# Both heads of a pair take their raw-score maxima from different row halves of TensorE, k gets eight slots, and the order is set anew

## The chip, the cores and the metric

One core of one Trainium2 chip runs the whole program. The metric is the device time of one execution in microseconds (us). TensorE multiplies matrices, VectorE and GpSimd do elementwise work and reductions, ScalarE does activations and copies, and SyncE issues the DMAs. In the profile these are PE (PEld for its weight loads), DVE, POOL, ACT and SP.

## The reference, cut to what matters

```python
def _attn_ref(q, k, v, g_q, g_k):                      # 4 batches, 12 heads, 448 rows, 64 wide
    q_n, k_n = (rmsnorm(q, g_q), rmsnorm(k, g_k))
    scores = scale * np.matmul(q_n, k_n.transpose(0, 1, 3, 2))
    scores = scores - np.max(scores, axis=-1, keepdims=True)
    attn = np.exp(scores)
    attn = attn / (np.sum(attn, axis=-1, keepdims=True) + 1e-09)
    return np.matmul(attn, v)

def reference(...):
    x = attn_out                        # as 1792 tokens by 768
    x = _moe_ref(x, phi, w1, w2)        # soft mixture of 8 experts, 4 slots each
    return _moe2_ref(x, w_in, w_out)    # h = x @ w_in; (h * sigmoid(1.702 h)) @ w_out
```

The change is in the attention alone. The experts and the last two products follow it and are the same in both kernels.

## The kernel before, in words

The 48 heads are worked through as 24 pairs of heads. Two pairs make a quad, which is what one load of q, k or v brings. For each pair `square` and `meansq` give the mean squares, `invert` gives 1/rms, `gain` and `normalise` scale q and k, and then each of q and k is split into a high and a low 16-bit half (`q_hi`, `q_lo`, `k_hi`, `k_lo`, with copies in `q_again` and `k_again`). A slot is 128 columns wide: 64 of them hold the high half of 64 numbers, the other 64 the low half or a helper. q has eight slots in a pair (four chunks of rows for each of two heads). k has seven: three full chunks for each head, and one slot in which the last 64 rows of both heads share the 128 partitions.

`turn` transposes such a tile by a DMA that SP issues. Pairs 0 and 1 use TensorE instead (`pe_turn`, `pe_copy`). After the transpose the 64 numbers of a high half lie on 64 of TensorE's 128 rows. The transposed tiles are KBT (k high and a -1), QAT (q high and low), KAT (k low and high) and QBT (q high and the maximum).

A pair is then handled in two steps. First `mx` multiplies the high halves of q and k, 64 rows deep, and `mx_max` takes the maximum over the 448 keys on VectorE, straight from PSUM. It works in groups: three groups of two chunks each (two matmuls of 128 columns against 448, into two PSUM banks, and one reduction over 2 x 448), and a fourth group for the last 64 rows of both heads, whose two matmuls of 64 columns write partitions 0 to 63 and 64 to 127 of one bank, with one reduction over 448. `mx_move` then carries the second head's maxima from partitions 64 to 127 down to 0 to 63. There is one PSUM buffer for these groups (`mx=1` in `BUFS`), so a group's matmuls wait until the reduction of the group before is done. Pair 0 takes its chunks one by one from the score buffers, in seven groups. Second, once the maxima are written into the q tile and that is transposed (`tqb`), `sc` makes the scores in two 128-row matmuls for each chunk, `sc_exp` exponentiates on ScalarE, `esum` adds for the denominators, and `pv`, `sums`, `xst` and `xmul` make the rows that the mixture of experts reads.

The order of all this is written by `run`, a planner inside the kernel: each step is an `op` with an engine, a cost and a due time, and the planner lists the steps on every engine when the program is built. The tables `ON` (which of DVE, POOL or ACT does a step of a pair, one letter for each pair), `SHIFT` (what is added to a due time) and `COST` steer it. On the chip each engine then runs its list in order, and waits at the head of the list for what the next step needs. Where the planner expects TensorE to be idle it puts in small filler matmuls (`warm`, line 366). Weights for the experts are loaded ahead during the attention (`early`), and into the attention's own buffers as these come free at its end (`ev`, `e0` to `e3`).

Around it stand the loads of the quads on SP (lines 372 and 376), the transposes on SP (line 472), the maxima on PE (line 506) and DVE (line 510), `mx_move` (line 517) and the scores (line 525).

Of the kernel before, what the change touches and what calls it, by code (L numbers as in the profile page):

```python
# [20 lines left out]
def soft_moe_block_kernel(  # L21
# [21 lines left out]
    C = 4  # L43
# [11 lines left out]
        gain="PPPPPDPDPPPPPPPPDDPDPPDD",  # L55
        qn="DPPPPDPPPPPPPPPPPPPDPPPP",
        kn="DPDDDDDDPPPDPPDDPDPDPPPP",
        qlo="PPPPPPPDPPPPPDPPDPDPDDDD",
        klo="PDPDPPPPPPDDPPPPPPDDPDDP",
        q2="DADPADADDPAAPDPAAAAADAAP",  # L60
        k2="DDDADAAADADAPPADDDPAAPPP",
        e01="DPPPPPPDPPDPPDPPDDPPDDDD",
        e02="DPPPDPPPPDPPDPDDDPDDDPPP",
        e11="PPPPPDDPDDPPDDPPPDPPPPPD",
        e12="PPPPPPPPPDPPDPPPDDDPDPPP",
        x0="DADDAAAAADDDAAAADDDDADDD",
        x1="AAADDDDDDAADAAAADDADDAAA",
        nr="DDDDPPPPPPPP",
# [137 lines left out]
    tmp_t = wr_t[0][:, 2048:3008].rearrange("p (a d) -> p a d", d=D)  # L206
# [22 lines left out]
    rings["rstd"] = [w3_t[:, 2976 + 32 * i:3006 + 32 * i] for i in range(2)]
# [25 lines left out]
        e0=2528.9, e1=-318.3, e2=1377.8, e3=-312.5, early=-356.6, esum=1121.5, ev=683.3, exp=101.7,  # L255
        gain=2452.3, guard=-280.1, invert=-347.4, k2=1399.8, khi=-233.2, klo=-1664.4, kn=1136.3, lk=404.5,
        logits=-430.7, lq=-148.4, max=32.7, meansq=-234, move=-828, mx=-239.9, out=-2170.8, pe_tka=-148.1,
        pe_tkb=-423.3, pe_tqa=279.8, pe_tqb=-458.7, pv=-92.3, q2=144.5, qhi=379.1, qlo=-547.3, qn=1645.5,
        r_add=1029.5, r_back=78.3, r_eb=512.8, r_exp=-422.8, r_fade=-274.5, r_gather=-1334.2, r_max=-104.7,
        r_more=-342.3, r_neg=51.3, r_old=-38.4, r_turn=-770.3, r_z=23.8, recip=-482, sc=149.1, square=-302.9,  # L260
        squarek=-1386.1, ssb=-423.4, sumT=-108.1, sums=-696.5, tka=1788, tka0=-596.3, tkb=-430.1, tkb0=981,
        tqa=-351.3, tqa0=-100.1, tqb=-605.9, tqb0=-2095.7, v=1218.9, w_back=-205.6, w_copy=-1379.6,
        w_exp=-467.5, w_guard=385.6, w_max=-49.2, w_neg=-638.7, w_recip=416.3, w_scale=1218.5, w_sel=-46.1,
        w_sum=1102.3, w_turn=-561.7, w_z=-432.7, x=1755.3, xmul=372.4,
    )
    COST = dict(
        gain=(0.6, 1.23), qn=(0.6, 1.02), kn=(0.53, 0.9), qlo=(0.6, 1.12), klo=(0.53, 1.0), q2=(0.2, 1.1, 0.52),
        k2=(0.19, 1.0, 0.47), e01=(0.53, 1.09), e02=(0.53, 1.09), e11=(0.53, 1.09), e12=(0.53, 1.09),
# [124 lines left out]
    def square(p, i):  # L393
        if i == 0:
            sqt[p] = tmp_t
        nc.scalar.activation(out=sqt[p][:, 8:] if i else sqt[p][:, :8], in_=rows(p, i), func=AF.Square, scale=D ** -0.5)  # L396

    def meansq(p):
        if p % 2 == 0:
            ssqt[p // 2] = new("ssq", [P, 30])  # L400
        nc.vector.tensor_reduce(out=part(ssqt, p, 1), in_=sqt.pop(p), axis=AX.X, op=ALU.add)

    def part(tiles, p, n):

        a = 15 * (p % 2)
        return tiles[p // 2][:, a:a + 15 * n]

    def invert(p, i, n):

        qd = p // 2  # L410
        if i == 0 and p % 2 == 0:
            y0t[qd], ntt[qd] = new("y0", [P, 30]), new("nt", [P, 30])
        if i == 5 and p % 2 == 0:
            rst[qd] = new("rstd", [P, 30])
# [19 lines left out]
    def rows(p, i):  # L434
        a = 8 * (p % 2)
        return of(raw_t, p // 2)[:, i, a:a + 8 - i]
# [7 lines left out]
    def normalise(p, i):  # L444
        n, eng, m = rows(p, i), on("kn" if i else "qn", p)[0], (8, 7)[i]
        r = part(rst, p, 1)[:, 8 * i:8 * i + m].rearrange("p (a o) -> p a o", o=1)
        eng.tensor_tensor(out=n, in0=n, in1=r.to_broadcast([P, m, D]), op=ALU.mult)  # L447
# [1039 lines left out]
```

## Time and profile before

| what | value |
|---|---|
| median of 3 runs | 692.09 us (691.33 to 695.41) |
| the profiled execution's own time | 693.83 us |
| its span | 692.1 us |
| mean granted TensorE clock, as a share | 0.968 |

The profiled execution is one more run than the three. Its time has 1.73 us around the span. The attention runs to about 300 us of the span, the experts to about 415 us, and the last two products to the end.

### The profile page before, as it was taken

To read this page: it belongs to the slowest core of one execution; us is meant where nothing else is said; L and a number is where in the kernel's file an instruction comes from. 1 tells how busy PE (TensorE), PEld (TensorE's weight loads), DVE (VectorE), ACT (ScalarE), POOL (GpSimd) and SP (SyncE) were. 2 spreads that over 40 slices of the span, in tenths; PEclk is the share of its full clock that TensorE was granted. 3 is DMA by queue.
4 is the path that set the end of the run, shared out by engine and by line. 5 is a ranking of instruction groups with operands and counts; after the bars stand their busy time and mean duration, and the time that the engine had idled before them with its cause. 6 is when DMAs were issued, how large, how long until landed. Compare 5 with 4: busy or idle time off the path is not lost.

```text
span 692.1 us, 11043 instructions
## 1 busy us (share of the span) xinstructions
PE 630.0 (91%) x4089; PEld 414.5 (60%) x4089; DVE 377.5 (55%) x640; ACT 365.8 (53%) x762; POOL 191.9 (28%) x233
## 2 busy tenths in 40 slices
PE   1889999999999999989743899999999999999997
PEld 0423434434433433455421335799999999999997
DVE  4997777877887888243544613799511211211211
ACT  2756977877787964532533511898513432333332
POOL 4756898776577353400000010000000000000000
PEclk9999999999999999988966899999999999999999
DMA  8289999898899899659899995663100100100101
GB/s 225 71 166 219 201 225 203 169 224 194 183 213 202 174 217 223 229 192 391 325 407 406 407 357 208 246 223 124 70 0 1 69 1 1 68 1 1 69 0 46
DMA packets 146166, 120.30 MB, mean 174 GB/s; under 512 B 102048, under 2 KB 126880, under 8 KB 146112
## 3 DMA queue, kind: packets, MB, share of 16 engines
q1 hardware_dynamic: 143024, 109.47, 57.7%
q10 hardware_dynamic: 3024, 10.03, 3.7%
q8 instruction: 32, 0.52, 0.3%
q14 instruction: 22, 0.18, 0.1%
q0 software_dynamic: 64, 0.10, 0.1%
HBM read 92.18 MB, written 5.51 MB: 141 GB/s over the span
## 4 chain that ended last, share of the span: by engine, by line
PE 74%; DMA 12%; DVE 9%; ACT 2%; issue 1%; SPq 1%; POOL 0%; ACTq 0%; DVEq 0%; POOLq 0%
PE y L1307 27%; PE y L1324 7%; PE sc L525 7%; PE pv L544 7%; PE mx L506 4%; DMA wr<-in_moe_w_dram 4%; PE pv L539 3%; DMA wr<-wr 3%; PE so_ps L1110 2%; PE h L1077 2%; DVE wr L510 2%; PE f L1266 2%; DMA wt<-in_moe_w_dram 2%; PE ms L591 2%; PE ms L590 1%; DVE wr L447 1%
## 5 line engine op out<-in xcount | busy, mean ns | idle before, releaser
L1288 DVE TENSOR_TENSOR gl<-gg,gh 128x384 fp32r<-128x384 f32 (+1 forms) x80 | 42.2, 530 | 149.1 <-ACT gh L1283 148.3
L510 DVE TENSOR_REDUCE wr<-mx 128x2 f16<-128x896 f32 x92 | 89.7, 975 | 25.5 <-PE mx L506 25.1
L1274 ACT ACTIVATE gg<-f 128x384 f32<-128x384 f32 (+1 forms) x78 | 36.5, 469 | 121.0 <-PE f L1266 120.8
L1307 PE MATMUL y<-wo,gh 128*128 128x384 f32 x352 | 75.4, 335 | 0.0
L532 POOL TENSOR_TENSOR es<-es,e 128x448 f32<-128x448 f32 x47 | 55.4, 1189 | 29.7 <-DVE es L532 12.1
L529 ACT ACTIVATE e<-sc,esc 128x448 f32<-128x448 f32 x96 | 56.6, 637 | 11.5 <-PE sc L525 10.6
L1307 PEld LDWEIGHTS y<-wo,gh 128*128 128x128 f32 x352 | 62.1, 188 | 0.0
L1307 PE MATMUL y<-wh,gl 128*128 128x384 f32 x176 | 46.8, 337 | 0.0
L1307 PE MATMUL y<-wl,gh 128*128 128x384 f32 x176 | 46.7, 336 | 0.0
L1307 PE MATMUL y<-wh,gh 128*128 128x384 f32 x176 | 46.7, 336 | 0.0
L1307 PE MATMUL y<-wo,gl 128*128 128x384 f32 x176 | 44.9, 335 | 0.0
L1283 ACT ACTIVATE gh<-gg 128x384 fp32r<-128x384 f32 (+1 forms) x78 | 39.3, 504 | 7.5 <-PE y L1307 4.2
L396 ACT ACTIVATE wr<-wr 128x512 f32<-128x512 f32 (+1 forms) x48 | 28.6, 604 | 26.5 <-DMA wr<-in_k_dram 12.6
L529 ACT ACTIVATE es<-sc,esc 128x448 f32<-128x448 f32 x54 | 32.9, 634 | 18.3 <-PE sc L525 18.1
L146 ACT ACTIVATE wi<-wst 128x512 f32<-128x512 f32 x24 | 16.2, 675 | 36.4 <-DMA wr<-in_moe_w_dram 15.7
L447 POOL TENSOR_TENSOR wr<-wr 128x512 f32<-128x512 f32 (+1 forms) x33 | 32.8, 1016 | 5.4 <-DVE wr L432 4.9
L525 PEld LDWEIGHTS <-wr 128*128 128x128 f16 (+1 forms) x224 | 18.9, 104 | 24.7 <-issue 17.6
L506 PE MATMUL mx<-wr 64*128 64x448 f16 (+1 forms) x120 | 31.0, 365 | 2.5 <-DVE wr L510 2.4
L143 DVE SCALAR_TENSOR_TENSOR wst<-wst 128x512 uint32<-128x512 uint32 x24 | 16.6, 691 | 28.8 <-ACT wst L149 26.3
L1307 PEld LDWEIGHTS y<-wl,gh 128*128 128x128 f32 x176 | 32.0, 188 | 0.0
L1307 PEld LDWEIGHTS y<-wh,gl 128*128 128x128 f32 x176 | 32.0, 188 | 0.0
L1307 PEld LDWEIGHTS y<-wo,gl 128*128 128x128 f32 x176 | 31.8, 188 | 0.0
(270 smaller groups left out, 1362.7 us busy)
## 6 DMA issues: line engine op xcount, KB each, us to landing
wr<-in_moe_w_dram SPq DMA_DIRECT2D x30, 512.0 KB, 8.7
wt<-in_moe_w_dram SPq DMA_DIRECT2D x24, 512.0 KB, 7.9
wr<-in_moe_w_out_dram SPq DMA_DIRECT2D x15, 768.0 KB, 4.5
wst<-in_moe_w_in_dram ACTq DMA_DIRECT2D x19, 512.0 KB, 7.4
wr<-in_moe_w_dram SPq DMA_DIRECT2D x20, 384.0 KB, 5.5
wt<-in_moe_w_dram SPq DMA_DIRECT2D x20, 384.0 KB, 7.8
out_dram<-o SPq DMA_DIRECT2D x13, 384.0 KB, 2.3
wr<-in_q_dram SPq DMA_DIRECT2D x12, 384.0 KB, 4.7
```

Source lines behind the costliest of these rows:

```text
L447: eng.tensor_tensor(out=n, in0=n, in1=r.to_broadcast([P, m, D]), op=ALU.mult)
L506: nc.tensor.matmul(out, q_cols(QAT[p], h, c)[:D], k_cols(KBT[p], h)[:D], start=True, stop=True)
L510: nc.vector.tensor_reduce(out=of(qb_t, p)[:, at[0]:at[-1] + 1:max(1, at[-1] - at[0]), D:D + 1], in_=MX.pop((p, g))[:, :len(at), :S], axis= ...
L525: nc.tensor.matmul(out, k_cols(a, n, c), q_cols(b, n), start=first, stop=not first)
L529: nc.scalar.activation(out=E[p, h, c], in_=SC.pop((p, h, c)), func=AF.Exp, scale=esc)
L532: on(f"e{h}{c}", p)[0].tensor_tensor(out=E[p, h, 0], in0=E[p, h, 0], in1=E[p, h, c], op=ALU.add)
L544: nc.tensor.matmul(PV[p][h * D:(h + 1) * D, :], t[:, 6 * n + 3 * h + c], E[p, h, c], start=(c == 0), stop=False)
L1274: nc.scalar.activation(out=ggt[w][:, :w[1]], in_=src[:, :w[1]], func=AF.Silu, scale=1.702)
L1283: nc.scalar.activation(out=gh[:, :w[1]], in_=ggt[w][:, :w[1]], func=AF.Copy)
L1288: nc.vector.tensor_tensor(out=G[w][1][:, :n], in0=ggt[w][:, :n], in1=G[w][0][:, :n].bitcast(F32), op=ALU.subtract)
L1307: nc.tensor.matmul(Y[t, u][:, :384], a[:, ts], b[f][:, u * 384:(u + 1) * 384], start=(f == 0 and i == 0), stop=(f == KF - 1 and i == 2),)
L1324: nc.tensor.matmul(Y[t, u][:, :384], a[:, t * 128:(t + 1) * 128], b[:, u * 384:(u + 1) * 384], start=(f == 0 and j == 0), stop=(f == KF - ...
```

## The change

All of q and k now has eight slots in a pair. The first head keeps its high half in columns 0 to 63 of a slot and its low half in 64 to 127; the second head has them the other way round (`lanes`). After the transposes the first head's high halves lie on rows 0 to 63 and the second head's on rows 64 to 127. A group of maxima (pairs 1 to 23) is now one chunk of both heads: two matmuls, one on each half of TensorE's rows, into two PSUM banks, and one reduction over 2 x 448. The last group has 64 rows of each head, on partitions 0 to 63, and reduces 2 x 448 too. `mx_move` goes. Pair 0 has eight groups of one chunk. k's tiles, squares and copies grow from 448 to 512 columns and its two transposed tiles from 7 to 8 blocks, and the short load of k becomes one DMA in a quad instead of two. Small tiles (1/rms and its helpers, the gain, the 16-bit identity) move to the buffer `wv`, so that the last of the `ev` loads waits for more steps and the last loads of `e2` and `e3` for fewer. The tables `ON`, `SHIFT` and `COST` have new numbers.

```diff
@@ ON, SHIFT, COST (one row of each shown) @@
-        kn="DPDDDDDDPPPDPPDDPDPDPPPP",
+        kn="DDPPDPDDPPDDDPDDDPDPPDPP",
-        logits=-430.7, lq=-148.4, max=32.7, meansq=-234, move=-828, mx=-239.9, out=-2170.8, pe_tka=-148.1,
+        lq=-482.3, max=3.6, meansq=-561.7, mx=-361.9, out=-2747.4, pe_tka=-741.5, pe_tkb=1475.9, pe_tqa=1239.5,
-        gain=(0.6, 1.23), qn=(0.6, 1.02), kn=(0.53, 0.9), qlo=(0.6, 1.12), klo=(0.53, 1.0), q2=(0.2, 1.1, 0.52),
+        gain=(0.6, 1.23), qn=(0.6, 1.02), kn=(0.6, 1.02), qlo=(0.6, 1.12), klo=(0.6, 1.12), q2=(0.2, 1.1, 0.52),
...
-        load(qd, k, t[:, :, :3], [(t[h * SH:(h + 1) * SH, 0:4:2, 3], slice(h, 4, 2)) for h in range(2)])
+        load(qd, k, t[:, :, :3], [(t[:SH, :, 3], slice(0, 4))])
...
-        return of(raw_t, p // 2)[:, i, a:a + 8 - i]
+        return of(raw_t, p // 2)[:, i, a:a + 8]
+    def heads(x):
+        return x.rearrange("p (h c) d -> p h c d", h=2)
+    def lanes(t, second):
+        at, step = (D, 448) if second else (0, 576)
+        flat = t.rearrange("p a d -> p (a d)")
+        return bass.AP(flat.tensor, flat.offset + at, [list(flat.ap[0]), [step, 2], [128, C], [1, D]])
...
-        nc.scalar.activation(out=of(kb_t, p)[:, :, 0:D], in_=rows(p, 1), func=AF.Copy)
+        nc.scalar.activation(out=lanes(of(kb_t, p), 0), in_=heads(rows(p, 1)), func=AF.Copy)
...
-        store[p] = new(tag, [128, a, P], F16)
+        store[p] = new(tag, [128, 8, P], F16)
...
-        chunks = [(0, 0), (0, 1), (0, 2), (1, 0), (1, 1), (1, 2), (0, 3)]
-        return [chunks[i:i + 2] for i in range(0, 7, 2)] if p else [[chunks[i]] for i in (0, 1, 2, 6, 3, 4, 5)]
+        if p:
+            return [[(0, c), (1, c)] for c in range(C)]
+        return [[(h, c)] for h in range(2) for c in range(C)]
...
-            for h in range(2) if c == 3 else (h,):
-                out = ps[SH * h:SH * h + SH, 0, :S] if c == 3 else ps[:, n, :S]
-                nc.tensor.matmul(out, q_cols(QAT[p], h, c)[:D], k_cols(KBT[p], h)[:D], start=True, stop=True)
+            r = slice(h * D, h * D + D)
+            a = cols(QAT[p], h, c)[r]
+            nc.tensor.matmul(ps[:a.shape[1], n, :S], a, cols(KBT[p], h)[r], start=True, stop=True)
...
-    def mx_move(p):
-        t = of(qb_t, p)
-        nc.vector.tensor_copy(out=t[:SH, 7, D:D + 1], in_=t[SH:, 3, D:D + 1])
...
-        ("ev", wv_t, NP - 7, [[], [], [], done(Z, "tkb", "klo", "k2")]),
+        ("ev", wv_t, NP - 7, [[], [], [("pe_tqb", 1)] + [("pe_" + x, 1) for x in ("tkb", "tqa", "tka")], done(Z, "tkb", "klo", "k2", "qn", "kn", "gain")]),
```

How this moves the instructions shows in the lists of the built programs. First VectorE in the start-up, around the maxima of pair 0 (`wr<-sc`); line 510 is 522 after the change, 281 is 284, 401 is 404, 440 is 452. Before:

```order
L281 COPY wr<-ms 128x384
L510 TENSOR_REDUCE wr<-sc 128x1 x3
L422 TENSOR_TENSOR wr<-wr 128x30
L281 COPY wr<-wr 128x7x64
L425 SCALAR_TENSOR_TENSOR wr<-wr 128x30
L510 TENSOR_REDUCE wr<-sc 128x1
L281 COPY wr<-ms 128x512
L517 COPY wr<-wr 64x1
L430 TENSOR_SCALAR wr<-wr 128x30
L510 TENSOR_REDUCE wr<-sc 128x1
L432 TENSOR_TENSOR wr<-wr 128x30
L510 TENSOR_REDUCE wr<-sc 128x1 x2
```

And after:

```order
L459 TENSOR_TENSOR wr<-wr 128x512 x2
L522 TENSOR_REDUCE wr<-sc 128x1 x3
L284 COPY wr<-ms 128x512
L522 TENSOR_REDUCE wr<-sc 64x1
L284 COPY wr<-ms 128x512
L522 TENSOR_REDUCE wr<-sc 128x1 x3
L522 TENSOR_REDUCE wr<-sc 64x1
L284 COPY wr<-wr 128x2x4x64
L452 TENSOR_TENSOR wr<-wr 128x512
L284 COPY kat_162<-ms 128x512
L404 TENSOR_REDUCE wr<-wr 128x16
```

Pair 0 has eight reductions instead of seven, `mx_move` (line 517) and the four small `invert` steps of the second quad (lines 422 to 432) have left VectorE's list here, and two products (a `gain`, line 452, and the normalising of line 459) stand in it.

Second TensorE after the last PV matmul of pair 0, where the maxima of pair 2 (`qat_154`, `kbt_163`) stand; line 506 is 517 after, 366 is 369, 525 is 533. Before:

```order
L366 LDWEIGHTS ident
L366 MATMUL ms<-ident 128x256
L539 MATMUL pv<-es_156,wr 128x448
L506 LDWEIGHTS qat_154
L506 MATMUL mx<-kbt_163,qat_154 128x448
L506 LDWEIGHTS qat_154
L506 MATMUL mx<-kbt_163,qat_154 128x448
L525 LDWEIGHTS kat_162
L525 MATMUL sc<-wr,kat_162 128x448
```

And after:

```order
L369 LDWEIGHTS ident
L369 MATMUL ms<-ident 128x256
L517 LDWEIGHTS qat_154
L517 MATMUL mx<-kbt_163,qat_154 128x448
L517 LDWEIGHTS qat_154
L517 MATMUL mx<-kbt_163,qat_154 128x448
L369 LDWEIGHTS ident
L369 MATMUL ms<-ident 128x256
```

Before, pair 1's scores (`kat_162`) follow at once. After, three runs of fillers (14, 10 and 4 matmuls) and two groups of pair 2's maxima stand between pair 1's last maxima and its first scores; before, 14 fillers stand in this part of the list in all (2, 6 and 6).

Third VectorE in the middle of the attention, around the last group of a pair. Before:

```order
L440 TENSOR_TENSOR wr<-wr 128x512
L447 TENSOR_TENSOR wr<-wr 128x448
L510 TENSOR_REDUCE wr<-mx 128x1
L517 COPY wr<-wr 64x1
L447 TENSOR_TENSOR wr<-wr 128x448
L510 TENSOR_REDUCE wr<-mx 128x2
```

And after:

```order
L459 TENSOR_TENSOR wr<-wr 128x512
L452 TENSOR_TENSOR wr<-wr 128x512
L522 TENSOR_REDUCE wr<-mx 128x2
L522 TENSOR_REDUCE wr<-mx 64x2
L404 TENSOR_REDUCE wr<-wr 128x16
L522 TENSOR_REDUCE wr<-mx 128x2
```

The short reduction and the move of a pair have become one reduction over two heads on 64 partitions.

Counted over the whole lists, VectorE loses 24 moves (line 517), has 21 normalising products of 512 columns instead of 12 of 448 and 3 of 512, 19 copies of half a tile instead of 16, 28 products for `xmul` instead of 24, one `esum` more and one `k_lo` less. TensorE has 72 fillers in and around the attention instead of 56. SP issues 24 short loads of q and k instead of 36.

## Rows read from the trace of the kernel before

**Rows 1.** The page: busy time of each engine, then tenths in 40 slices
```profile
PE 630.0 (91%) x4089; PEld 414.5 (60%) x4089; DVE 377.5 (55%) x640; ACT 365.8 (53%) x762; POOL 191.9 (28%) x233
...
PE   1889999999999999989743899999999999999997
...
PEclk9999999999999999988966899999999999999999
DMA  8289999898899899659899995663100100100101
```
**Rows 2.** Busy time by stretch: the attention's middle, and the experts
```profile
core 0: us, PE busy (x) PEld busy (x) DVE busy (x) ACT busy (x) POOL busy (x), PEclk, DMA share, GB/s
70.00:280.00 210.00, 208.04 (x1157) 84.73 (x1155) 167.50 (x256) 157.02 (x357) 141.38 (x159) 1.00 0.93 202
315.00:420.00 105.00, 74.81 (x849) 34.75 (x841) 42.81 (x85) 34.82 (x66) 3.44 (x17) 0.84 1.01 382
```
**Rows 3.** What PE waited for, 70 to 280 us
```profile
PE mx L506 <- DVE wr L510: 1.6, 5, 0.5
```
**Rows 4.** Busy time of line 506 alone, 70 to 280 us (PE, then PEld)
```profile
70.00:280.00 210.00, 38.70 (x154) 9.10 (x154) 1.00 0.93 202
```
**Rows 5.** PE in order of time around two groups of maxima: start, duration, what
```profile
162.37 0.55 PE L506 MATMUL mx<-wr 64*128 64x448 f16 x2
162.85 0.97 PE L544 MATMUL pv<-e,v 128*64 128x448 f32 x4
163.75 1.02 PE L539 MATMUL pv<-es,v 128*128 128x448 f32 x2
164.70 0.38 PE L506 MATMUL mx<-wr 64*64 64x448 f16 x2
165.01 0.36 PE L525 MATMUL sc<-wr 128*128 128x448 f16 x1
```
**Rows 6.** VectorE's groups, 0 to 315 us: count, busy and mean ns, idle before
```profile
L510 DVE TENSOR_REDUCE wr<-mx 128x2 f16<-128x896 f32 x69 | 75.4, 1093 | 19.9 <-PE mx L506 19.7
L401 DVE TENSOR_REDUCE wr<-wr 128x15 f32<-128x960 f32 x24 | 27.5, 1145 | 6.2 <-ACT wr L396 4.7 <-POOL wr L440 1.3
L510 DVE TENSOR_REDUCE wr<-mx 128x1 f16<-128x448 f32 x23 | 14.3, 621 | 5.5 <-PE mx L506 5.3
L447 DVE TENSOR_TENSOR wr<-wr 128x448 f32<-128x448 f32 x12 | 12.6, 1067 | 0.1
L607 DVE TENSOR_TENSOR xl<-ms,rs 128x384 f32<-128x384 f32 x22 | 12.1, 553 | 12.5 <-PE ms L591 12.2
L440 DVE TENSOR_TENSOR wr<-wr 128x512 f32<-128x512 f32 x7 | 5.7, 808 | 1.2 <-ACT wr L396 1.2
L517 DVE COPY wr<-wr 64x1 f16<-64x1 f16 x24 | 3.6, 151 | 0.8
L447 DVE TENSOR_TENSOR wr<-wr 128x512 f32<-128x512 f32 x3 | 2.4, 784 | 0.0
L281 DVE COPY wr<-wr 128x512 f16<-128x512 f16 x7 | 2.8, 406 | 0.0
```
**Rows 7.** The DMA queues while transposes alone are under way, 154.5 to 157 us
```profile
DMA packets 1922, 0.48 MB, mean 191 GB/s; under 512 B 1922, under 2 KB 1922, under 8 KB 1922
```
**Rows 8.** The DMA queues, 70 to 280 us
```profile
DMA packets 98500, 42.35 MB, mean 202 GB/s; under 512 B 82724, under 2 KB 95012, under 8 KB 98482
```
**Rows 9.** The chain that ended last, 16 to 40 us: start, us, what
```profile
25.19 1.59 DVE wr L510 x3
...
36.93 1.10 DVE wr L510
```
**Rows 10.** The same chain, among the experts
```profile
341.63 8.99 DMA wr<-in_moe_w_dram
...
357.49 11.72 DMA wr<-in_moe_w_dram
```
**Rows 11.** PE in order of time: the first score of pair 1
```profile
45.20 0.36 PE L525 MATMUL sc<-wr,kat 128*128 128x448 f16 x1
```

More of the change, by code (lines that the diff above doesn't have):

```diff
@@ L54, in soft_moe_block_kernel @@
     ON = dict(
[L55 to L68 removed]
+        gain="DPPPDPPPPPPPPPDDDPPDPPPD",
+        qn="DDPPPDPPPPPPPPPDDPDPPDPD",
+        kn="DDPPDPDDPPDDDPDDDPDPPDPP",
+        qlo="PPPPPPPDPPPPPDPPDPDDPDDD",
+        klo="DPPDPPPPPPPDPDPPPPDDPPDP",
+        q2="DPPDADADDDAADDPAAPDDADDA",
+        k2="PDPADAAADADPPAAPPDAADDAA",
+        e01="PPPPPPPDPPDPPDPPPDPPDDDD",
+        e02="DPPPDPPPPDDPPPPPPDPPPDDD",
+        e11="PPPPPDDPDPDDDDPPDPPPDDPD",
+        e12="DPPPPPPPPDDPDPPPDPDPDPPD",
+        x0="DADAAAADADDDDDADAADDAAAD",
+        x1="DAADDDDDDAADAADDDDDDDADA",
+        nr="DPPDPPPPDPDD",
     )
@@ L260, in soft_moe_block_kernel @@
[L260 to L264, printed above, removed]
+        e0=259.6, e1=926.4, e2=-434, e3=-1647, early=-1468.4, esum=911.3, ev=407.8, exp=170.9, gain=2447.7,
@@ L395, in square @@
             sqt[p] = tmp_t
-        nc.scalar.activation(out=sqt[p][:, 8:] if i else sqt[p][:, :8], in_=rows(p, i), func=AF.Square, scale=D ** -0.5)
+        nc.scalar.activation(out=sqt[p][:, 8 * i:8 * i + 8], in_=rows(p, i), func=AF.Square, scale=D ** -0.5)
     def meansq(p):
         if p % 2 == 0:
-            ssqt[p // 2] = new("ssq", [P, 30])
+            ssqt[p // 2] = new("ssq", [P, 32])
         nc.vector.tensor_reduce(out=part(ssqt, p, 1), in_=sqt.pop(p), axis=AX.X, op=ALU.add)
     def part(tiles, p, n):
-        a = 15 * (p % 2)
-        return tiles[p // 2][:, a:a + 15 * n]
+        a = 16 * (p % 2)
+        return tiles[p // 2][:, a:a + 16 * n]
     def invert(p, i, n):
@@ L524, in sc @@
                 out = ps[SH * n:SH * n + SH] if c == 3 else ps
-                nc.tensor.matmul(out, k_cols(a, n, c), q_cols(b, n), start=first, stop=not first)
+                nc.tensor.matmul(out, cols(a, n, c), cols(b, n), start=first, stop=not first)
     def sc_exp(p, h, c):
@@ L692, in soft_moe_block_kernel @@
                 ("tqb", p), "SP", 1.32, t - 4, lambda p=p: turn(p, "qbt", QBT, lambda: of(qb_t, p)),
-                sub("q2", "move") + [("max", p, g) for g in range(len(gs))], ("qbt", p),
+                sub("q2") + [("max", p, g) for g in range(len(gs))], ("qbt", p),
             )
@@ L699, in soft_moe_block_kernel @@
                     ("pe_tqb", h), "PE", 0.22, t - 4.1, lambda h=h, tag=tag: pe_turn(tag, lambda: qb_t[0], 4 * h, 4 * h + 4),
-                    sub("q2") + [("max", p, i) for i in range(4 * h, 7 if h else 4)] + (sub("move") if h else []), g[0],
+                    sub("q2") + [("max", p, i) for i in range(4 * h, 4 * h + 4)], g[0],
                 )
```

117 lines of the change are left out of this document (60 added, 57 removed).

## The prediction

> **What bounds the kernel now.** I read the page first: TensorE is busy 91% of the span, and in its slices the attention (to about 300 us) and the last products are full, with a hole among the experts where the DMA line is full instead [rows 1]. A busy TensorE can hide small stalls, so the next view is what it waited for in the attention's middle, 70 to 280 us. There is one row: five waits of 1.6 us in total [rows 3]. In that stretch TensorE is busy 208 of 210 us at a granted clock of 1.00, VectorE 167.5 (80%), ScalarE 157.0 (75%), GpSimd 141.4 (67%), and the DMA share is 0.93 [rows 2]. So there TensorE sets the pace, and what is taken off it counts until another engine is reached.
>
> The pace follows from line 506. It has 154 matmuls in the stretch [rows 4], a pair has eight, so 19.25 pairs pass in 210 us: 10.9 us for a pair. VectorE's 167.5 us are then 8.7 us for a pair.
>
> The start-up is different. From 16 to 40 us the chain that ended last runs over VectorE's reductions and products [rows 9], so there VectorE's list sets the time. Among the experts the chain stands on weight loads of 9 and 12 us [rows 10] at a DMA share of 1.01 [rows 2]. The last of these loads go into buffers that the attention frees at its end, so an attention that ends earlier lets them start earlier by as much, and I take what the attention gains or loses as passed on in full. The other end is that the experts are held by something else and keep all of it, so that nothing is gained; against it, the loads that the chain shows are those that follow the attention's end.
>
> **TensorE's part, the gain.** The view in order of time gives what a group of maxima takes until the next work starts [rows 5]. Two matmuls of 128 columns start at 162.37 and the next line at 162.85: 0.48 us, one after the other. The group of 64-column matmuls, whose outputs lie on different partitions, starts at 164.70 and the next line at 165.01: 0.31 us, so these two run side by side. Before, a pair pays 3 x 0.48 + 0.31 = 1.75 us. If two matmuls on different halves of the rows run side by side as those on different columns do, a pair pays 4 x 0.31 = 1.24 us. That is 0.51 us less for each of 23 pairs: 11.7 us. No row of this trace shows two row halves at once, so the other end is 4 x 0.48 = 1.92 us, 0.17 more for a pair, +3.9 us in all. I take the side-by-side value, because the row with column halves is the nearest one and the two outputs lie in different banks.
>
> The Trainium skill speaks to this in "TensorE: Matmul & The Clock Gate", section "Part 3: Packing small matmuls": matmuls in distinct row groups start within about 4 ns of each other. By it the sum stays at 11.7 us; no run here shows it yet.
>
> **VectorE's part, the price.** The durations are from the groups of VectorE [rows 6]. The short group becomes a long one: 1.093 - 0.621 = +0.472 us for a pair, on 64 partitions but over the same 896 numbers. The move goes: -0.151. `meansq` reads 1024 instead of 960: 1.145/15 = +0.076. The normalising products go from 12 of 1.067 and 3 of 0.784 to 21 that I put at 0.9, between the two rows: 18.9 - 15.2 = 3.7 us over 24 pairs, +0.16. Three more copies at 0.406 and four more `xmul` at 0.553 give 3.4 us, +0.14. Together +0.70 us: VectorE goes from 8.7 to 9.4 us for a pair, while TensorE goes to 10.9 - 0.51 = 10.4. So VectorE is not the bound, but is busy 90% instead of 80%. Its list is worked in order: behind a maximum that waits stand products and sums for later pairs, and behind these the next maxima, which TensorE waits for through the one PSUM buffer. At 80% this cost TensorE 1.6 us in 19 pairs [rows 3]. What it costs at 90% no row shows. The low end is nothing; the high end is that VectorE takes back all that TensorE saves, 11.7 us. I take 2 us, much nearer to the row.
>
> **The DMA's part.** k's two transposes grow from 7 to 8 blocks. While transposes alone are under way the queues move 1922 packets in 2.5 us [rows 7]: 769 in a microsecond. Of 98500 packets in the middle 82724 are small [rows 8]; over 19.25 pairs that is 4300 for a pair. A block is 128 x 128 numbers of 16 bits, 32 KB, and at 0.48 MB for 1922 packets, 250 bytes each, it has 128 packets. Two blocks more are 256 packets, 0.33 us for a pair, 7.3 us of queue time over the 22 pairs that use them. The share was 0.93 of 10.9 = 10.1 us for a pair, and would be 10.5 at a pace of 10.4. Taken as a hard limit at 1.00 this costs 0.1 us for each of 22 pairs, 2 us; but the same count reaches 1.01 among the experts, and in 93% there are packets that only wait for memory, so the low end is nothing. I take 1 us. SP saves twelve issues of short loads, which I put at nothing: SP is not in the chain here; if SP were late it would be a gain of under 0.6 us in a quad.
>
> **The start-up.** Here VectorE's list counts, not TensorE's. Up to the last maximum of pair 1 the list gains one reduction of pair 0 (+0.62), the longer last group of pair 1 (+0.47), a `gain` of 0.81 twice (+1.6), 0.076 six times in `meansq` (+0.5), and a `k_lo` that I put at the 1.07 of the normalising product; it loses two moves (-0.3), four small steps of `invert` (-0.6, put at the 0.15 of the move) and two copies (-0.8). That is +2.5 us. On TensorE's list 28 fillers stand between pair 1's last maxima and its first scores, where before 14 stood in the whole part, which says that a wait is expected there. Fillers that run in a wait cost nothing. The low end is -1 us, if the earlier scores of pair 0's first head let its PV end sooner; the high end is +5, if pair 1's transposed maxima also come late. I take +2.5.
>
> **The edits that I cost at nothing.** The longer squares and copies of k lie on ScalarE, which is busy 75% and loses 16 `xmul` pieces; without that cover they are under 0.1 us a pair. The later release of the last `ev` load and the earlier one of `e2` and `e3` lie in a stretch of many loads; a late one would cost a load of 9 us at most once, and I keep that in the upper end. The new due times have no price of their own beyond the waits above.
>
> **The sum**, against the profiled execution's 693.8 us: -11.7 + 2.0 + 1.0 + 2.5 = -6.2, so 687.6. The profiled execution stands 1.7 us above the median of the runs shown, so against that median I forecast 692.1 - 6.2 = 685.9, rounded to 686.
>
> **Rivals.**
> First, the waits do not come: TensorE keeps its pace with VectorE at 90%, and the start-up is as before. Then -11.7 gives 680.4. For it speaks that TensorE waited only 1.6 us at 80%; against it, the start-up's chain.
> Second, VectorE takes TensorE's place. It has the longer reductions and 90% of the time, and most of its idle time before the maxima is waiting for line 506 (19.7 us [rows 6]), which shrinks as the groups get shorter. If each in-order wait for another engine now delays a maximum, the pace stays at 10.9 us, the 11.7 are gone and the start-up stays: 692.1 + 2.5 = 694.6. Against it: 9.4 is still 1.0 us below 10.4. The Trainium skill has this as a rule in "TensorEngine Tiling (Array Packing)", section "PSUM Bottleneck": tiling speeds up TensorE but not the emptying of PSUM. The trace agrees so far that a reduction of 1.09 us stands behind matmuls of 0.31 to 0.48.
> Third, and slower: the two halves of the rows do not run side by side. A group then costs 0.48, a pair 0.17 more than before, +3.9 us; with the start-up of 2.5 and 0.5 us of further waits the time is 699.0. It decides from the point where two matmuls of one group start 0.2 us apart instead of almost together. For it speaks only that the trace has no such pair; against it, the column halves do it.
>
> **How the numbers follow.** The forecast's own case has 0.50, from 682 to 691 by its bounds; the full gain 0.20; VectorE in TensorE's place 0.20; row halves in turn 0.10. Faster by over 1% is below 685.2 (1% is about what a measurement of this kernel can tell from no change). The full gain is wholly there, and a little less than half of the forecast's case: 0.20 + 0.23 = 0.43. Slower by over 1% is above 699.0: half of the third rival and the tail of the second, with a start-up at its high end and a late weight load, 0.05 + 0.06 = 0.11. The rest, 0.46, is the same. The range goes from 678, a little past the full gain (start-up at -1 and a quicker last group), to 697, which takes in the second rival with its start-up at +5 and leaves out the third.
>
> **What would show it right or wrong.** In the profile after, two matmuls of a group start nearly together and a group takes about 0.31 us; the mean pace between 70 and 280 us is near 10.5 us; VectorE is busy near 90% there; TensorE's waits for VectorE are a few us, not ten; the DMA share is above 0.95; the first scores of pair 1 come one to three microseconds later than at 45.2 us [rows 11]. The prediction is wrong if the pace stays near 10.9 with TensorE waiting (second rival), if a group takes 0.48 (third), or if the attention ends earlier and the experts do not.

## The result, and the profile after

| | kernel before | changed kernel |
|---|---|---|
| median of 12 runs | 692.02 us (688.97 to 695.47) | 696.63 us (692.99 to 700.03) |
| ratio | 1 | 1.0058 (95% interval 1.0034 to 1.0083) |
| the profiled execution's time, its span | 693.83 us, 692.1 us | 694.15 us, 692.2 us |

The change makes the kernel 0.6% slower, 4.0 us by the ratio. The forecast was 686, 0.9% faster: the direction was wrong. The range (678 to 697) holds the result by 0.4 us, at the end that was set for the second rival, so that is luck and not the sum. The two profiled executions are further apart from their medians than from each other (1.8 us above it and 2.5 us below), so the traces show where time moves inside the attention, not the whole 4 us; prices are taken from the ratios.

TensorE in order of time in the changed kernel, around two groups of maxima (answers to [rows 5]):

```profile
160.34 0.38 PE L517 MATMUL mx<-wr 64*64 64x448 f16 x2
160.65 1.02 PE L547 MATMUL pv<-wr,v 128*128 128x448 f32 x2
...
163.02 0.37 PE L517 MATMUL mx<-wr 64*128 64x448 f16 x2
163.32 0.33 PE L598 MATMUL ms<-ident,ot 128*128 128x128 f32 x1
```

The group of 128 columns starts at 163.02 and the next line at 163.32: 0.30 us where it took 0.48. Read singly from the trace, the two matmuls of a group start 3 ns apart (199 ns before). So the row halves run side by side, as forecast. Line 517 alone in the attention's middle (answers to [rows 4]), then busy time by stretch (answers to [rows 2]):

```profile
70.00:280.00 210.00, 27.49 (x150) 8.54 (x150) 1.00 0.97 205
```

```profile
70.00:280.00 210.00, 201.50 (x1168) 83.04 (x1166) 182.30 (x262) 155.32 (x338) 134.59 (x137) 1.00 0.97 205
315.00:420.00 105.00, 71.40 (x825) 33.39 (x817) 42.65 (x85) 34.49 (x65) 3.44 (x17) 0.84 1.03 390
```

150 matmuls are 18.75 pairs: the pace is 210 / 18.75 = 11.2 us for a pair, where the prediction had 10.4 in place of 10.9. A window of this length cuts through pairs at both ends; between two marks of the work itself (the table below) the stretch is as long as before, 231.3 us against 230.8. TensorE's busy time falls from 208.0 to 201.5 us and no more pairs pass: it waits. The seven longest of its waits in this stretch (answers to [rows 3]; the view lists only gaps of more than 0.15 us):

```profile
PE mx L517 <- DVE wr L522: 1.5, 3, 0.9
PE sc L533 <- ACT e L537: 1.3, 2, 0.8
PE ms L598 <- ACT xl L611: 0.9, 1, 0.9
PE mx L517 <- DMA kbt<-wr: 0.9, 1, 0.9
PE ms L598 <- DVE pacc L833: 0.8, 1, 0.8
PE mx L517 <- DVE xl L615: 0.6, 1, 0.6
PE pv L552 <- ACT ot L555: 0.6, 2, 0.4
```

These are many small waits for VectorE, ScalarE and DMA. Only the first stood in the trace before, and it was no smaller there (1.6 us in five waits); the others are new. VectorE has 182.3 us, 87% of the stretch, 9.7 us for a pair. Its reductions (answers to [rows 6], 0 to 315 us):

```profile
L522 DVE TENSOR_REDUCE wr<-mx 128x2 f16<-128x896 f32 x69 | 75.2, 1090 | 19.9 <-PE mx L517 19.5
L404 DVE TENSOR_REDUCE wr<-wr 128x16 f32<-128x1024 f32 x24 | 29.1, 1214 | 6.7 <-ACT wr L399 5.4 <-POOL wr L540 1.2
L522 DVE TENSOR_REDUCE wr<-mx 64x2 f16<-64x896 f32 x23 | 24.9, 1084 | 2.9 <-PE mx L517 2.8
```

The last group's reduction over 64 partitions takes 1.08 us, as long as one over 128: 24.9 us where 14.3 and 3.6 for the moves stood. And the first score of pair 1 (answers to [rows 11]) comes 3.1 us later:

```profile
48.27 0.35 PE L533 MATMUL sc<-wr,kat 128*128 128x448 f16 x1
```

### The profile page after: what moved, and what is told of

Same layout as the page of the kernel before. It is cut to its first block, busy times and chain, and to the rows that moved or that the text cites. A ratio compares the mean times of both kernels' runs of the same rounds, so it can differ in the third digit from the quotient of the medians.

```text
span 692.2 us, 11045 instructions
## 1 busy us (share of the span) xinstructions
PE 616.3 (89%) x4109; PEld 410.7 (59%) x4109; DVE 393.9 (57%) x634; ACT 364.2 (53%) x744; POOL 187.8 (27%) x221
## 4 chain that ended last, share of the span: by engine, by line
PE 68%; DMA 12%; DVE 9%; ACT 5%; issue 2%; SPq 1%; POOL 1%; ACTq 0%; DVEq 0%; POOLq 0%
PE y L1314 27%; PE y L1331 7%; PE pv L552 6%; PE sc L533 6%; DMA wr<-in_q_dram 3%; PE so_ps L1117 3%; DMA wt<-in_moe_w_dram 3%; PE mx L517 3%; PE pv L547 2%; PE h L1084 2%; DVE wr L522 2%; PE f L1273 2%; DMA qbt<-wr 1%; DMA wr<-in_k_dram 1%; DMA wst<-in_moe_w_in_dram 1%
## 5 line engine op out<-in xcount | busy, mean ns | idle before, releaser
L522 DVE TENSOR_REDUCE wr<-mx 128x2 f16<-128x896 f32 x92 | 100.1, 1088 | 22.8 <-PE mx L517 22.3
L1314 PE MATMUL y<-wo,gh 128*128 128x384 f32 x352 | 75.4, 335 | 0.0
L540 POOL TENSOR_TENSOR es<-es,e 128x448 f32<-128x448 f32 x45 | 52.4, 1173 | 33.2 <-PE pv L552 16.1
L399 ACT ACTIVATE wr<-wr 128x512 f32<-128x512 f32 x48 | 29.7, 629 | 17.0 <-DVE wr L973 5.5
L404 DVE TENSOR_REDUCE wr<-wr 128x16 f32<-128x1024 f32 x24 | 29.1, 1214 | 6.7 <-ACT wr L399 5.4
L459 POOL TENSOR_TENSOR wr<-wr 128x512 f32<-128x512 f32 x27 | 29.8, 1125 | 8.2 <-DVE wr L435 5.5
L1107 PE MATMUL t<-ident,hs 128*128 128x128 f32 x16 | 4.0, 337 | 31.5 <-DVE hTz L1112 29.5
```

Of the source, the lines that this page charges most:

```text
L399: nc.scalar.activation(out=sqt[p][:, 8 * i:8 * i + 8], in_=rows(p, i), func=AF.Square, scale=D ** -0.5)
L459: eng.tensor_tensor(out=n, in0=n, in1=r.to_broadcast([P, 8, D]), op=ALU.mult)
L522: nc.vector.tensor_reduce(out=lanes(of(qb_t, p), 1)[:m, h:h + n, c, 0:1], in_=MX.pop((p, g))[:m, :n, :S], axis=AX.X, op=ALU.max,)
L540: on(f"e{h}{c}", p)[0].tensor_tensor(out=E[p, h, 0], in0=E[p, h, 0], in1=E[p, h, c], op=ALU.add)
L1314: nc.tensor.matmul(Y[t, u][:, :384], a[:, ts], b[f][:, u * 384:(u + 1) * 384], start=(f == 0 and i == 0), stop=(f == KF - 1 and i == 2),)
```

## The experiments

In every trace I added up TensorE's matmul records between two marks: the first score of pair 4, and the last eight matmuls of `r_gather`, with which the attention ends. "Work" is the time from one start to the next; where the next start is later than the modelled end, the rest is "idle", short gaps included. Times are microseconds, ratios are to the kernel before.

| kernel | pair 1's first score | pair 4's | last gather | work | idle | ratio (95%) |
|---|---|---|---|---|---|---|
| before | 45.2 | 77.1 | 307.9 | 226.3 | 4.5 | 1 |
| changed | 48.3 | 78.3 | 309.6 | 220.8 | 10.6 | 1.0058 (1.0034 to 1.0083) |
| b_halves | 45.9 | 77.1 | 302.8 | 217.1 | 8.6 | 0.9942 (0.9916 to 0.9968) |
| b_long | 45.0 | 77.7 | 310.4 | 226.3 | 6.5 | 1.0069 (1.0048 to 1.0089) |
| b_halves_long | 46.6 | 78.3 | 308.6 | 218.3 | 12.0 | 1.0014 (0.9988 to 1.0040) |
| b_halves_light | 44.4 | 75.5 | 302.0 | 216.6 | 9.9 | 0.9921 (0.9896 to 0.9946) |
| b_halves_dma | 45.6 | 75.4 | 301.1 | 217.7 | 7.9 | 0.9899 (0.9875 to 0.9922) |
| b_halves_both | 45.4 | 75.1 | 301.0 | 216.3 | 9.6 | 0.9852 (0.9817 to 0.9886) |
| b_both | 44.4 | 75.5 | 304.1 | 225.4 | 3.2 | 0.9940 (0.9921 to 0.9959) |
| b_late | 48.9 | 81.0 | 310.4 | 225.4 | 3.9 | 1.0076 (1.0050 to 1.0102) |
| b_halves_late | 47.3 | 79.4 | 304.4 | 217.6 | 7.4 | 0.9988 (0.9963 to 1.0012) |
| a_halfmax | 48.6 | 77.7 | 306.0 | 219.8 | 8.6 | 0.9989 (0.9971 to 1.0006) |
| a_last | 48.0 | 79.5 | 310.0 | 221.9 | 8.6 | 1.0047 (1.0027 to 1.0067) |
| a_k7 | 48.1 | 77.9 | 308.4 | 221.9 | 8.6 | 1.0065 (1.0043 to 1.0086) |
| a_start | 49.2 | 79.9 | 313.4 | 223.6 | 9.9 | 1.0117 (1.0085 to 1.0148) |
| a_start2 | 44.2 | 78.1 | 311.4 | 221.0 | 12.2 | 1.0072 (1.0045 to 1.0099) |

Theory at the start: TensorE's saving is real and is lost to VectorE's list. Rivals: it is lost to the DMA queue; it is lost at the start; or a TensorE that was full to 99% gives up time only as far as the other engines' lists stand ready.

**The row halves alone (b_halves).** The kernel before with its own order; only the second chunk of a group uses the other half of the rows, where the same tile holds other numbers.

```diff
+            r = slice(D, 2 * D) if p and n else slice(0, D)
-                nc.tensor.matmul(out, q_cols(QAT[p], h, c)[:D], k_cols(KBT[p], h)[:D], start=True, stop=True)
+                nc.tensor.matmul(out, q_cols(QAT[p], h, c)[r], k_cols(KBT[p], h)[r], start=True, stop=True)
```

> The kernel before, in its own order and with its own tables; in groups of two chunks the second chunk's matmul takes rows 64 to 127 of both transposed tiles instead of rows 0 to 63, so that the two matmuls run on different row halves. The maxima of the second chunks are then those of other numbers; the softmax is the same for any value subtracted. Nothing else is changed: VectorE, the DMAs and the lists are those of before. Theory 1 (TensorE set the pace of the kernel before, and the change lost its gain through what it added): 23 pairs x 3 groups x 0.17 us = 11.7 us off, 680 to 682. Theory 2 (another engine or the DMA stood right behind TensorE in the kernel before): 688 to 692, with TensorE waiting more.

688.25 us, a ratio of 0.9942: 4.0 us faster, and so faster than both kernels (its maxima of the second chunks are those of other numbers, so it prices the row halves and is no version to keep). In the table work falls by 9.2 us (the maxima's matmuls alone from 32.3 to 22.3) and idle rises by 4.1, so that the attention's end gains 5.1. What TensorE waited for, 70 to 280 us:

```profile
PE mx L507 <- DVE wr L511: 2.4, 7, 0.5
PE sc L526 <- ACT e L530: 1.1, 1, 1.1
PE mx L507 <- DMA wr<-wr: 0.8, 1, 0.8
PE ms L567 <- ACT ssb L562: 0.4, 1, 0.4
PE mx L507 <- DMA qat<-wr: 0.4, 1, 0.4
```

Not even with every other engine's list unchanged do 10 us of TensorE become 10 us of time.

**VectorE's length alone (b_long) and with the halves (b_halves_long).** The last group's reduction reads its 448 columns twice.

```diff
+        if p and g == 3:
+            nc.vector.tensor_reduce(
+                out=of(qb_t, p)[:, 3:8:4, D:D + 1], in_=MX.pop((p, g))[:, :1, :S].to_broadcast([P, 2, S]), axis=AX.X, op=ALU.max,
+            )
+            return
```

> The kernel before, where only the last group's reduction of pairs 1 to 23 reads its 448 numbers twice (896), as long as the changed kernel's. VectorE has 0.47 us more for a pair, 10.9 us in all; the rest is as before. Theory VectorE (its longer list delays TensorE through waits in order): 697 to 703. Theory not VectorE: 692 to 694, start-up +0.5.

> b_halves with the last reduction of each pair from pair 1 on reading its 448 columns twice (as b_long; the result is the same): 0.47 us a pair more on VectorE, 10.9 in all. If the length of VectorE's list is what the changed kernel loses by, this comes near it: 693 to 696, a ratio of 1.002 to 1.006, with TensorE idle for some 12 us from pair 4 to the last gather (8.6 in b_halves). If VectorE has room beside the shorter TensorE list, 688 to 690 (0.994 to 0.997), and the loss lies in the new order and its start.

10.9 us more on VectorE cost 4.8 us on the kernel before (0.9942 to 1.0014 is 5.0 us on b_halves, each with some 2 us either way). Both times lie a little below what was expected if VectorE's length decides (697 and a ratio of 1.002 at the least). The idle of the second run is the 12 us expected. Its longest waits, 70 to 280 us:

```profile
PE mx L507 <- DVE wr L516: 5.2, 9, 1.2
PE mx L507 <- DVE wr L512: 1.7, 2, 1.3
```

6.9 us in place of b_halves' 2.4: a group waits for the reduction before it, through the one PSUM buffer. The changed kernel has the same length in an order made for it, and there this wait is 1.5 us; so the run prices the length in the old order, and not in the changed kernel.

**Relief on b_halves (b_halves_light, b_halves_dma, b_halves_both) and without the halves (b_both).** Shorter reductions, fewer transposed blocks, both.

```diff
-            in_=MX.pop((p, g))[:, :len(at), :S], axis=AX.X, op=ALU.max,
+            in_=MX.pop((p, g))[:, :len(at), :S // 2 if p else S], axis=AX.X, op=ALU.max,
...
-        nc.sync.dma_start_transpose(out=store[p], in_=src().rearrange("p a d -> p (a d)"))
+        n = 7 if tag[0] == "q" else 6
+        nc.sync.dma_start_transpose(out=store[p][:, :n], in_=src()[:, :n].rearrange("p a d -> p (a d)"))
...
```

> The kernel before with its second chunks on rows 64 to 127 (as b_halves), and each reduction of the maxima reads 224 of its 448 columns from pair 1 on (the maxima of the other columns are left out): VectorE is relieved of some 38 us, TensorE's list is that of b_halves. b_halves was worth 3.8 us where its matmuls gave up 10 to 11 us. If VectorE takes the rest back, most of it appears here: 682 to 684, a ratio of 0.985 to 0.988, and TensorE's waits for VectorE in the pairs are at most what they were in the kernel before (4 us). If VectorE isn't what takes it, the time stays at 687 to 689. Between them, 685 to 686: VectorE takes about half of it and the rest lies elsewhere.

> b_halves with fewer blocks in the DMA transposes: k's take 6 of 7, q's 7 of 8 from pair 2 on (the last block of each, that is the second head's last chunk and for k half of the chunk before it, stays zero and is left out), 4 of 30 blocks of a pair. If the DMA queue is what holds b_halves back (busy share 0.95), the time falls by the same part as with VectorE's relief, to 683 to 685 (ratio 0.987 to 0.990) and the busy share to 0.88. If it isn't, 687 to 689, as b_halves.

> b_halves with both reliefs: reductions over 224 of 448 columns and k's and q's transposes a block shorter (the same parts left out as in b_halves_light and b_halves_dma). In the stretch from pair 1's first score to the last gather b_halves gained 5 us of the 10 that TensorE gave up, and neither relief alone gave more (256.4, 257.3 and 255.1 us). If VectorE and the DMA queue together hold it, the stretch falls to 250 to 252. If the waits come of the order, in which each engine's list is fixed and was fitted to a longer TensorE list, it stays at 254 to 256, and the time is 681 to 684, from the start and the experts' weights alone.

> The kernel before with both reliefs and without the row halves (same parts left out). If TensorE bounds its pairs, the reliefs are worth next to nothing there: from pair 1's first score to the last gather 260 to 262 us as in the kernel before (262.1), and whatever the time gains (2 to 6 us) lies ahead of pair 1 or in the experts. If VectorE or the DMA queue bounds a part of the pairs already, the stretch falls to 257 or less.

The times fall (by 1.5, 3.0 and 6.2 us against b_halves), but not where a bound would give way. From pair 4 to the last gather b_halves takes 225.7 us, and with the reliefs 226.5, 225.7 and 225.9; idle stays at 8 to 10. So b_halves_dma, whose time is the one expected if the queue held it, doesn't show that it does. Without the halves both reliefs bring 2.2 us there (230.8 to 228.6). Some of the gain lies ahead of pair 4 (75.1 to 75.5 against 77.1), the rest behind the attention or in no trace: the profiled execution of b_halves_both took 685.37 us, 4.0 above that kernel's median. Busy time of the stretch 70 to 280 us with both reliefs shows how much room was made:

```profile
70.00:280.00 210.00, 202.83 (x1188) 86.26 (x1187) 141.58 (x255) 158.51 (x366) 146.25 (x162) 1.00 0.92 197
```

VectorE at 67% and TensorE still waits. So VectorE's load does not hold back b_halves in the pairs. Nor does what the DMA relief took away, but that was little: the share goes from 0.95 to 0.89 alone and 0.92 with both. I put the rest to the order: each engine's list is fixed, and was fitted to a longer TensorE list. That is what is left over, not shown by a list fitted anew, and a rival stands beside it. In b_halves_both the chain that ended last stands on the loads of q and k for 26.6 of the 210 us (5.0 in the kernel before), and no run made these arrive earlier; nor did one relieve ScalarE (75%) or GpSimd (70%).

**The changed kernel with shorter reductions (a_halfmax, a_last) and one block less (a_k7).**

```diff
-            in_=MX.pop((p, g))[:m, :n, :S], axis=AX.X, op=ALU.max,
+            in_=MX.pop((p, g))[:m, :n, :S // 2 if p else S], axis=AX.X, op=ALU.max,
```

> The changed kernel, where each reduction of pairs 1 to 23 reads only the first 224 of 448 columns, so that VectorE has about 0.5 us less for each of 92 groups, some 43 us; order, matmuls and DMAs are the same. It leaves out half of the maxima's input. Theory VectorE (its list is what took TensorE's gain): 682 to 687. Theory DMA or order: 694 to 697.

a_last, with one reduction for the last rows of both heads:

```diff
+            out = ps[n * SH:n * SH + SH, 0, :S] if p and c == 3 else ps[:a.shape[1], n, :S]
...
+        if p and c == 3:
+            nc.vector.tensor_reduce(out=t[:, 0:1, 3, 0:1], in_=MX.pop((p, g))[:, :1, :S], axis=AX.X, op=ALU.max)
+            nc.vector.tensor_copy(out=t[:SH, 1, 3, 0:1], in_=t[SH:, 0, 3, 0:1])
+            return
```

> The changed kernel with its own order; the last chunks of the two heads (64 rows each) go to output partitions 0 to 63 and 64 to 127 of one bank, one reduction over 448 columns takes both in place of 896, and a copy of 64x1 moves the second head's maxima back, as the kernel before does it. VectorE gets back about 0.47 us a pair less the copy's 0.1, some 8 us in 23 pairs. If VectorE's longer reductions are what the change loses by, at the 0.43 us of time for 1 us of work that b_long showed, the time falls by 3 to 4 us: 692.5 to 694, a ratio of 1.000 to 1.003. If they lie beside other work: 696 to 697, 1.005 to 1.007.

```diff
-        nc.sync.dma_start_transpose(out=store[p], in_=src().rearrange("p a d -> p (a d)"))
+        n = 8 if tag[0] == "q" else 7
+        nc.sync.dma_start_transpose(out=store[p][:, :n], in_=src()[:, :n].rearrange("p a d -> p (a d)"))
...
```

> The changed kernel, where the DMA transposes of k move 7 of the 8 blocks, as before the change; the eighth block holds zeros, so the second head's last 64 keys are left out. The order is the same. It takes away 256 packets for each of 22 pairs, 7.3 us of queue time. Theory DMA (the added blocks took the gain): 686 to 690. Theory VectorE or order: 695 to 697.

Some 43 us off the reductions (34 off VectorE's busy time from 0 to 315 us) give 4.8 us back (1.0058 to 0.9989), the 7 us that a_last takes off the reductions give 0.8, which is within the intervals: less than b_long made me expect, and a_halfmax lies between the two times that I had named. As far as these runs go, adding length to a list costs more than taking the same length out of a list whose order was made around it gives back. The added blocks cost nothing that shows; the intervals leave room for 2 us, and in the trace of a_k7 the last gather comes 1.2 us earlier.

**The tables of before on the changed kernel (a_oldtables).** `ON` and `SHIFT` as they were.

> The changed kernel ordered by the numbers of before (the letters that choose an engine and the shifts of the due times). If the refit is what puts pair 1's first score 3 us later (48.3 against 45.2), it comes back here to 45 or 46 us, and the time to 693 to 695 unless the pairs run worse. If the eight reductions of pair 1, or its work in front of them, are the cause, it stays at 48 and the time is that of the changed kernel or above it (696 to 702), since the numbers don't fit.

730.41 us, a ratio of 1.0573 (1.0536 to 1.0609), with pair 1 at 45.0 us but pair 2 at 64.2 (54.9 before). Without the refit the change would cost 40 us, a time far above both that I had named: an order belongs to the lengths it was fitted to. Pair 1's first score is back at the time of before, with the longer reductions in front of it, so its 3 us belong to the new order. What that is worth this run can't tell, since the pairs behind it fall apart.

**The start (a_start, a_start2, b_late, b_halves_late).** a_start takes 15 steps of pairs 1 and 2 earlier in the planned list and leaves the rest as it is; three of its moves, each before the step named second:

```diff
+        (("pe_tqa", 1), ("sc", 0, 0, 0)),
+        (("max", 1, 3), ("meansq", 5)),
+        (("tqb", 1), ("tkb", 3)),
```

> The changed kernel with its own order but for the start: 15 instructions of pairs 1 and 2 are taken earlier (the transposes of pair 1's q before pair 0's scores, its four groups and their reductions in front of the squares' sums of pairs 4 and 5, the low part of pair 2's q ahead of two others on GpSimd, its DMA transposes and pair 1's ahead of those of k), and 20 fillers on TensorE go. If the late start is what it costs by the order alone, pair 1's first score comes at 42 to 45 us (48.3 in the changed kernel), pair 2's at 53 to 57 (61.4), and the time falls by about as much as pair 2's or 3's score, 2 to 4 us: 692.5 to 694.5, a ratio of 1.001 to 1.004. If the pairs behind it are paced by another engine from the start, the gain is gone by pair 8 (119.4) and the time is that of the changed kernel, 696 to 697.

The time rises, to 698.65 us, above all that was expected. The maxima of pair 1 come 4 us earlier (the transpose behind them is issued at 41.45 instead of 45.31 us), its scores later. TensorE in order of time, then VectorE:

```profile
44.03 0.36 PE L547 MATMUL mx<-kbt,qat 64*128 64x448 f16 x2
48.72 0.56 PE L547 MATMUL mx<-kbt,qat 64*128 64x448 f16 x2 [4.32 <-DVE wr L552]
49.21 0.56 PE L563 MATMUL sc<-wr,kat 128*128 128x448 f16 x1
49.55 0.58 PE L563 MATMUL sc<-qbt,wr 128*128 128x448 f16 x1
49.93 0.58 PE L563 MATMUL sc<-wr,kat 128*128 128x448 f16 x1
```

```profile
44.06 0.66 DVE L570 TENSOR_TENSOR wr<-wr,e 128x448 f32<-128x448 f32 x1
47.03 0.63 DVE L570 TENSOR_TENSOR wr<-wr,e 128x448 f32<-128x448 f32 x1 [2.31 <-POOL wr L570]
47.57 1.09 DVE L552 TENSOR_REDUCE wr<-mx 128x2 f16<-128x896 f32 x1
```

Read from below: pair 1's score stands behind pair 2's second group on TensorE; that group waits for the reduction of the first (47.57); the reduction stands behind an addition for pair 0 (47.03); and that waits for GpSimd. Three lists, each in order, and one step moved without the others gains nothing. Combined with a_last (a_start_last) the ratio was 1.0141 (1.0108 to 1.0175), no better.

```diff
+        (("esum", 0, 1, 2), ("q2", 3)),
+        (("sc", 1, 0, 0), ("mx", 2, 1)),
+        (("sc", 1, 1, 0), ("mx", 2, 1)),
```

> a_start with three more steps moved: pair 0's second addition on VectorE goes behind pair 2's first two reductions (it waited 2.3 us for GpSimd in front of them), and pair 1's first two score tiles go ahead of pair 2's second group on TensorE (which waited 4.3 us for VectorE). Pair 1's first score should come at 44.5 to 46 us (49.2 in a_start, 48.3 in the changed kernel). If the late start is part of the loss, the time falls by about 3 us against the changed kernel: 692.5 to 694.5 (ratio 1.001 to 1.004). If the pairs behind lose it again, as in a_start, 696 to 698.

Now pair 1's first score comes at 44.2 us, ahead of the kernel before, yet pair 2's at 60.0 (61.4 in the changed kernel) and pair 4's at 78.1 (78.3): the 4 us are gone by then. So in the changed order it is not pair 1 that sets the start; by what is left it is the preparation of pairs 2 to 4, which no run took by itself. What a late start costs was then measured on the other order:

```diff
+        for _ in range(7 if p == 1 and g == 3 else 1):
+            nc.vector.tensor_reduce(
...
```

> The kernel before with the last reduction of pair 1 done seven times (six more of 448 columns, the result is the same): some 3.2 us more on VectorE at that place and nowhere else, so that pair 1's maxima and the steps behind them come 3 us later. If a late pair 1 passes on whole, the time is 694.5 to 696 (ratio 1.004 to 1.006), and every pair's first score stands 3 us later to the end. If the pairs make it up: 691.5 to 693 (0.999 to 1.002).

> The same delay in b_halves, where TensorE waits some 9 us in the pairs. If a late start is absorbed there by those waits, the time stays at b_halves' 687 to 689 (ratio 0.993 to 0.995). If it passes on, 690.5 to 692 (0.998 to 1.000), and then the start alone takes three quarters of what the halves gained.

Pair 4's first score 3.9 us later puts the last gather 2.5 us later; on b_halves 2.3 give 1.6. (The granted clock of b_late from 20 to 50 us is 0.89, where the kernel before has 1.00, so some of the 3.9 us are slower matmuls.) By the ratios it is 5.3 us (above the range expected) and 3.2, with some 2 us either way. So by the traces some two thirds of a late start pass on to the attention's end, and a TensorE with room takes up no more of it than a full one.

## Why the prediction was wrong

| term | forecast | measured |
|---|---|---|
| TensorE's shorter groups | -11.7 | -4.0 (b_halves) |
| VectorE busier | +2.0 | +5.0 (b_halves_long against b_halves, 10.9 us of length) |
| two more blocks in a pair | +1.0 | nothing that shows (a_k7) |
| start-up | +2.5 | 3.3 by the trace, about 3 by what is left of the ratios |
| sum | -6.2 | +4.0 (the changed kernel) |

**The failed step is the sentence "what is taken off it counts until another engine is reached".** It read TensorE's 208 of 210 us as a bound with the others at a distance: VectorE at 80%, the DMA at 0.93. The matmuls did give up what was worked out (10.0 us from pair 4 on, by 32.3 to 22.3; 11.7 was the sum over 23 pairs). But b_halves shows that only 4 us of it reach the time with VectorE still at 80% and the DMA at 0.95, and b_halves_both that this doesn't change at 67% of VectorE. The other engines' average shares said nothing of how closely their single steps stood behind TensorE's: its 1.6 us of waits [rows 3] told how often others were later, not by how little they were earlier.

The chain that ended last tells this, and the prediction read it for the start and the experts only [rows 9, rows 10]. In the kernel before, from 70 to 280 us, it runs over TensorE for 155 of the 210 us, over DMAs for 28 and over VectorE for 21, and only 27 of the 38.7 us of line 506 stand in it. Its five longest pieces from 50 to 300 us (start, us, what):

```profile
130.85 4.72 DMA wr<-wr
188.27 4.06 DMA wr<-wr
194.78 5.04 DMA wr<-in_q_dram
208.44 5.19 DMA kat<-wr
218.35 5.29 DMA wr<-wr
```

In such a stretch TensorE had other work and hardly waited, but the step behind it hung on the transpose or the load, so by this chain a shorter TensorE list gains nothing there. TensorE's part of the 210 us falls to 121 in b_halves and 69 in b_halves_both, and rises to 188 in b_both. The chain is inferred from one execution of each kernel; a list fitted anew for b_halves, or earlier loads, which would test it, was not tried.

**The second failed term is VectorE's price.** The length was right (0.70 us a pair forecast, 16 us in 23 pairs; VectorE's busy time from 0 to 315 us rises from 235.2 to 251.8). Taken as 2 us, "much nearer to the row", it was 5.0 for the 10.9 us that b_halves_long adds: nearly half of the length. The other 5 us of the 16 no run took alone. The row to which it was held, 1.6 us of waits at 80%, came from a TensorE that was always busy; beside a shorter TensorE list in the old order the reductions are waited for (6.9 us). In the changed kernel they are waited for 1.5 us and a_last gave back 0.8, so how much of its loss is VectorE's length, and how much the new order, no run shows.

**The DMA's term** was inside its bounds (0 to 2) as far as the intervals tell. **The start-up** was sized about right: pair 1's first score came 3.1 us later ("one to three"). At pair 4 the changed kernel is 1.2 us later and has six `pv` and six `xst` matmuls more still to do (286 and 270 against 280 and 264 in b_halves, where one takes 0.25 and 0.11 us: 2.1 us), together 3.3. But the reason given, VectorE's list up to pair 1's maxima, was wrong: a_oldtables has pair 1's first score at 45.0 us with the same longer reductions, and a_start2 brought it to 44.2 and the time stayed.

**The rivals.** The second, VectorE in TensorE's place at 694.6, came out nearest: the stretch got no shorter, and TensorE waited. Its mechanism was half of it. In-order waits took back what the groups gained, as it said, but only part of them are waits for VectorE (in the changed kernel's seven rows above 1.5, 0.8 and 0.6 of 6.6 us). The Trainium skill's rule in "TensorEngine Tiling (Array Packing)", section "PSUM Bottleneck", that tiling speeds up TensorE and not the emptying of PSUM, is borne out by the changed kernel and b_halves_long: the reduction still takes 1.09 us behind a group that takes 0.30 in place of 0.48. The third rival fell: the starts are 3 ns apart, and so the trace agrees with the Trainium skill's "TensorE: Matmul & The Clock Gate", section "Part 3: Packing small matmuls", by which they lie within 4 ns.

The attention's end adds up: 1.2 us later at pair 4, 5.5 less work, 6.1 more idle is 1.8, and the last gather is 1.7 us later. Behind it the experts took 1.6 us back in the profiled execution (the first matmul of the last product, `y`, at 437.03 against 436.94), so that passing on in full, as I assumed, holds only roughly (in b_halves, 5.1 us ahead at the last gather, the same matmul comes 5.4 us earlier). Where the rest of the 4 us by the ratio arises the two profiles don't show.

## What to carry to other kernels

A busy share of 99% doesn't say what a saving on that engine is worth. Before a saving is counted, ask how early the others' results come, and read the chain of that very stretch and not only the waits; in this kernel of fixed in-order lists a third to a half of it arrived (4.0 of 11.7 us by the ratio, 5.1 of 10.0 in the table), and the cheapest test is to shorten the bound alone, with everything else as it was. Price a longer step on a second engine by the list it stands in (here nearly half of its length, at a share of only 80 to 85%), and keep the reductions over half the partitions out: 64 partitions cost as much as 128. An order refitted for new lengths is not one part of a change but the ground under it, and in a_start 15 steps moved by hand only moved the wait to the next list.

## What the runs showed of the hardware

After the wait of 4.3 us in a_start the granted clock fell. Busy time by stretch (the number before the DMA share is the clock):

```profile
44.00:48.60 4.60, 0.40 (x3) 0.11 (x3) 2.29 (x4) 1.12 (x2) 4.43 (x7) 1.00 0.93 239
48.60:52.00 3.40, 3.28 (x10) 0.92 (x10) 2.75 (x5) 1.44 (x3) 2.31 (x4) 0.52 0.70 159
52.00:56.00 4.00, 4.00 (x23) 1.28 (x21) 2.43 (x3) 3.81 (x8) 1.95 (x2) 0.98 0.77 217
```

While TensorE idles the clock still reads 1.00; in the 3.4 us of work that follow it is 0.52, the lower of its two levels (1.2 of 2.4 GHz), and the score matmuls take 0.56 us instead of 0.35. The changed kernel has 28 filler matmuls between 43.2 and 48.4 us and keeps 1.00. In a_start's rows above the scores start 0.34 to 0.38 us apart, where 0.19 is usual at the full clock: by my estimate the ten matmuls of that stretch lose some 1.7 us (half of 3.4) to one wait, besides the wait. And a reduction's time goes by what a partition reads, not by how many partitions read: 1084 ns over 64 and 1090 over 128, for the same 896 numbers.
